# A decode block on one core: 4 MB loads in 5 slots, K^T stationary for the scores, stationary gate, up and down weights

## The chip, the cores and the metric

The kernel runs on one core of one Trainium2 chip. The metric is device time in microseconds (us), the median of repeated executions; lower is better. The runs of one kernel lie within about 0.3% of each other except for a few outliers. A profiled execution gives the trace. Its span, from the first to the last instruction, is some 1.8 us shorter than the measured time (before: 419.2 and 420.96).

Engines in the profile: PE is the matrix engine and PEld its loading of stationary operands, DVE and ACT are the vector and scalar engines, POOL is GpSimd, SP issues the large DMA transfers. The core has 16 DMA engines, and a transfer to all 128 partitions is spread over all 16 by its partitions.

## The reference

One token (`x`: 1 x 1024) goes through layer norm, attention over a cache of 65,536 positions with 32 query heads and 4 K/V heads of 128, an output projection with a residual, a second layer norm and a gated FFN with a residual.

```python
def _A_ref(x, k_cache, v_cache, wq, wo):            # k_cache, v_cache: 1 x 4 x 65536 x 128
    q = (x @ wq).reshape(1, 1, 32, 128).transpose(0, 2, 1, 3)
    k = jnp.repeat(k_cache, 8, axis=1); v = jnp.repeat(v_cache, 8, axis=1)
    p = softmax(jnp.einsum("bhqd,bhkd->bhqk", q, k) * 128 ** -0.5)
    o = jnp.einsum("bhqk,bhkd->bhqd", p, v)
    return o.transpose(0, 2, 1, 3).reshape(1, 1, 4096) @ wo
h  = x + _A_ref(layernorm(x), ...)
n  = layernorm(h)
h2 = h + (gelu(n @ w_gate) * (n @ w_up)) @ w_down   # 1024 -> 3584 -> 1024
```

Everything is bf16 in memory. K and V are 134 MB, all weights together 39 MB, and each byte is used once.

## The kernel before

Loads go through one pool of nine 2 MB slots. For every 1 MB of K ("chunk", 32 rows per partition) PE transposes the data as pairs of bf16 in 16 fp32 transposes, DVE and ACT copy the result out, and the scores are computed with the small query as stationary operand and K^T streaming by. The scores then lie along the free dimension and have to be transposed back.

```python
def k_chunk_QK(g, ci):
    ...
    for par in range(2):
        for c in range(NBK):                         # 8 matmuls, K^T moving, 512 columns each
            mv = kts[c][:]...rearrange("p (b k t) -> p b k t", b=NB2, t=2)
            nc.tensor.matmul(qk_ps[32 * c:32 * c + 32, :], lhsT=qsel[:, g, par, :], rhs=mv[:, :, :, par],
                             start=(par == 0), stop=(par == 1), tile_position=(0, 32 * c))
    nc.scalar.copy(out=qk_sb[:], in_=qk_ps[:])
    for b in range(NB2):                             # 4 transposes back
        nc.tensor.transpose(out=sct_ps[:, b, :], in_=qk_sb[:, b * P:(b + 1) * P], identity=ident_f[:])
    ...
```

The V products of head group g - 1 are issued between the chunks of K of group g. The FFN streams the weights past a small stationary operand, gets rows, and turns each row into columns by splitting it into a high and a low bf16 part and multiplying both by a vector of ones:

```python
for which, wmat in ((0, B_w_gate), (1, B_w_up)):
    ...
            wide_mm(r_ps, hnz, c0 + cc, DC, ...)     # weights moving, 512 columns
    ...
    nc.vector.tensor_tensor(out=g_lo[:, sl], in0=r_ps[s][:, 0:fw[s]], in1=g_hi[:, sl], op=ALU.subtract)
    for part in (g_hi, g_lo):
        for f in range(FC):                          # 2 x 28 matmuls turn the row
            nc.tensor.matmul(gu_ps[:, which, f:f + 1], lhsT=part[:, f:F:FC], rhs=ones_bf[:, 0:1], ...)
```

The down projection does the same for 16 of its 28 column blocks, and computes the other 12 with the weights stationary, the last one from a 256 KB load of its own.

## Time and profile before

| before | |
|---|---|
| time | 420.96 us (3 runs, 420.91 to 422.46) |
| span of the profiled run | 419.2 us |
| bytes loaded | 173.02 MB |
| DMA engines held by the load queue | 97.7% of the span |
| PE busy | 79% |

The windows view of before, cut to DMA. The columns are the stretch, its length, busy time of POOL (not used here), the clock granted to PE as a share of full speed (PEclk), the mean DMA share and GB/s.

```profile
core 0: us, POOL busy (x), PEclk, DMA share, GB/s
240.00:300.00 60.00, 0.00 (x0) 0.97 1.01 427
400.00:404.00 4.00, 0.00 (x0) 0.86 1.01 426
404.00:408.00 4.00, 0.00 (x0) 0.50 0.91 380
408.00:412.00 4.00, 0.00 (x0) 0.50 0.51 209
```

The 16 engines do not end together: the share falls to 0.91 and then to 0.51 over the last 8 us. The timeline of before shows what follows the last loads (start, length, what):

```profile
399.49 4.27 DVE L399 TENSOR_TENSOR g_lo<-gu_row_ps,g_hi 128x512 bf16<-128x512 f32 x7
...
403.81 1.94 PE L402 MATMUL gu_ps<-ones_bf,g_lo 128*128 128x1 bf16 x28 [2.18 <-DVE g_lo L399]
...
407.52 3.62 PE L340 MATMUL d_ps<-wd_sb,actz 128*32 128x512 bf16 x32 [1.76 <-issue]
...
413.41 2.70 PE L447 MATMUL dl_ps<-act_bf,wd_sb 128*128 128x1 bf16 x96
...
417.09 0.36 SPq L482 DMA_DIRECT2D out_dram<-o_row  x1
```

After the last up weights PE and DVE need until 407.5 us to have the operand of the down projection, and the down projection then goes on until 416.1. The last 2.1 us are the store. The last 96 matmuls start without a wait: in before it is this chain on PE and DVE, not the last load, that ends last.

### The profile page before, as it was taken

The numbers are of one execution on the slowest core, as the hardware profiler recorded it, in microseconds if no ns is written. First come the engines' busy times: TensorE is split into PE (matmuls) and PEld (weight loads), VectorE is DVE, ScalarE is ACT, GpSimd is POOL, SyncE is SP. The second block draws the span as 40 slices with busy tenths as digits, with TensorE's granted clock in tenths as the row PEclk, the third lists the DMA queues.
The fourth block names the chain that finished last, engine by engine and source line by source line (L and its number), as shares of the span: only waits on it lengthen the run. The fifth ranks groups of instructions, "written<-read, shape, count | busy, mean of one in ns | idle before, by whom it ended". The sixth has DMA issues, their size and how long they took to land.

```text
span 419.2 us, 7313 instructions
## 1 busy us (share of the span) xinstructions
PE 330.3 (79%) x3085; PEld 215.5 (51%) x3085; DVE 184.8 (44%) x370; ACT 187.2 (45%) x318; POOL 5.0 (1%) x15
## 2 busy tenths in 40 slices
PE   3339999997898887988889879898886674678845
PEld 2337676655555554655655555555563231434443
DVE  3014666662644564555554565545554010016162
ACT  1007676738565453845656555555563600001100
POOL 2000000000000000000000000000000100000000
PEclk9999999996999999899999989999999585557775
DMA  8999999999999999999999999999999999999991
GB/s 323 423 428 432 424 424 428 428 427 428 427 427 425 425 428 430 430 423 424 428 427 430 428 421 430 424 425 433 424 427 424 428 428 427 413 421 419 430 401 62
DMA packets 13840, 173.48 MB, mean 414 GB/s; under 512 B 1392, under 2 KB 1392, under 8 KB 3696
## 3 DMA queue, kind: packets, MB, share of 16 engines
q1 hardware_dynamic: 13792, 173.02, 97.7%
q8 instruction: 24, 0.39, 0.4%
q14 instruction: 8, 0.07, 0.0%
q10 hardware_dynamic: 16, 0.00, 0.0%
HBM read 173.02 MB, written 0.00 MB: 413 GB/s over the span
## 4 chain that ended last, share of the span: by engine, by line
PE 48%; DMA 19%; ACT 14%; DVE 13%; issue 4%; SPq 0%; ACTq 0%; DVEq 0%
PE kt_ps L193 22%; PE sct_ps L222 9%; PE qk_ps L216 8%; ACT kt_sb L199 7%; DMA wgu_sb<-in_B_w_up_dram 7%; DMA k_sb<-in_A_k_cache_dram 6%; DMA wo_sb<-in_A_wo_dram 6%; PE acc_ps L275 4%; DVE sc_sb L225 4%; ACT pT L255 4%; DVE kt_sb L201 3%; ACT qk_sb L219 3%; DVE mx L226 3%; DVE g_lo L399 1%; PE d_ps L340 1%
## 5 line engine op out<-in xcount | busy, mean ns | idle before, releaser
L199 ACT COPY kt_sb<-kt_ps 128x1024 bf16<-128x1024 bf16 x116 | 116.1, 1013 | 106.4 <-PE kt_ps L193 106.0
L193 PE MATMUL kt_ps<-ident_f,k_sb 128*128 128x128 f32 x1024 | 143.3, 286 | 11.5 <-DVE kt_sb L201 8.8
L193 PEld LDWEIGHTS kt_ps<-ident_f,k_sb 128*128 128x128 f32 x1024 | 117.3, 146 | 34.6 <-DVE kt_sb L201 16.0
L201 DVE COPY kt_sb<-kt_ps 128x1024 bf16<-128x1024 bf16 x140 | 94.3, 686 | 53.1 <-PE kt_ps L193 52.7
L225 DVE COPY sc_sb<-sct_ps 128x256 f32<-128x256 f32 x64 | 38.9, 608 | 72.7 <-PE sct_ps L222 72.5
L216 PE MATMUL qk_ps<-kt_sb,qsel 128*32 128x512 bf16 x512 | 66.5, 395 | 4.7 <-ACT kt_sb L199 3.8
L222 PE MATMUL sct_ps<-ident_f,qk_sb 128*128 128x128 f32 x256 | 41.7, 284 | 12.4 <-ACT qk_sb L219 9.6
L219 ACT COPY qk_sb<-qk_ps 128x512 f32<-128x512 f32 x64 | 37.7, 590 | 27.2 <-PE qk_ps L216 27.2
L222 PEld LDWEIGHTS sct_ps<-ident_f,qk_sb 128*128 128x128 f32 x256 | 27.3, 141 | 34.9 <-ACT qk_sb L219 27.5
L275 PE MATMUL acc_ps<-v_sb,pT 128*32 128x512 bf16 x512 | 42.7, 426 | 0.7 <-DMA v_sb<-in_A_v_cache_dram 0.7
L255 ACT ACTIVATE pT<-sc_sb,nbias 128x256 bf16<-128x256 f32 x64 | 31.5, 495 | 14.4 <-DVE nbias L248 14.4
L216 PEld LDWEIGHTS <-qsel 128*32 128x32 bf16 x512 | 15.9, 94 | 31.0 <-issue 26.7
L226 DVE TENSOR_REDUCE mx<-sc_sb 128x8 f32<-128x256 f32 x64 | 26.7, 417 | 1.6
L275 PEld LDWEIGHTS <-pT 128*32 128x32 bf16 x512 | 13.8, 104 | 17.2 <-issue 10.2
L340 PE MATMUL gu_row_ps<-wgu_sb,hnz 128*32 128x512 bf16 x112 | 20.7, 485 | 2.1 <-DVE hnz L332 1.5
L152 PE MATMUL q_ps<-xn_bf,wq_sb 128*128 128x1 bf16 x256 | 7.5, 165 | 13.6 <-DMA wq_sb<-in_A_wq_dram 13.6
L396 ACT CAST g_hi<-gu_row_ps 128x512 bf16<-128x512 f32 x6 | 3.1, 594 | 32.5 <-PE gu_row_ps L340 32.5
L340 PE MATMUL at_ps<-wo_sb,o2z 128*32 128x512 bf16 x64 | 7.6, 626 | 9.9 <-DMA wo_sb<-in_A_wo_dram 9.9
L340 PEld LDWEIGHTS <-hnz 128*32 128x32 bf16 x112 | 8.1, 114 | 12.8 <-issue 7.2
L152 PEld LDWEIGHTS <-wq_sb 128*128 128x128 bf16 x256 | 7.1, 104 | 13.9 <-DMA wq_sb<-in_A_wq_dram 13.9
L349 ACT COPY at_r<-at_ps 128x512 f32<-128x512 f32 x1 | 0.6, 586 | 30.4 <-PE at_ps L340 30.4
L394 DVE CAST g_hi<-gu_row_ps 128x512 bf16<-128x512 f32 x8 | 5.0, 684 | 19.8 <-PE gu_row_ps L340 19.8
(121 smaller groups left out, 109.9 us busy)
## 6 DMA issues: line engine op xcount, KB each, us to landing
k_sb<-in_A_k_cache_dram SPq DMA_DIRECT2D x32, 2048.0 KB, 23.3
v_sb<-in_A_v_cache_dram SPq DMA_DIRECT2D x32, 2048.0 KB, 22.9
wq_sb<-in_A_wq_dram SPq DMA_DIRECT2D x4, 2048.0 KB, 14.3
wo_sb<-in_A_wo_dram SPq DMA_DIRECT2D x4, 2048.0 KB, 24.5
wgu_sb<-in_B_w_gate_dram SPq DMA_DIRECT2D x4, 1792.0 KB, 32.4
wgu_sb<-in_B_w_up_dram SPq DMA_DIRECT2D x4, 1792.0 KB, 31.8
wd_sb<-in_B_w_down_dram SPq DMA_DIRECT2D x3, 2048.0 KB, 30.6
wd_sb<-in_B_w_down_dram SPq DMA_DIRECT2D x1, 768.0 KB, 32.1
```

Of the source, the lines that this page charges most:

```text
L152: nc.tensor.matmul(q_ps[:, h:h + 1], lhsT=w_sb[:, h * P:(h + 1) * P], rhs=xn_bf[:, c:c + 1], start=False, stop=False, skip_group_check=True)
L193: nc.tensor.transpose(out=kt_ps[:, b, :], in_=k32[:, n0:n0 + 2, :].rearrange("p t d -> p (t d)"), identity=ident_f[:])
L199: nc.scalar.copy(out=dst_bf, in_=src_bf)
L201: nc.vector.tensor_copy(out=dst_bf, in_=src_bf)
L216: nc.tensor.matmul(qk_ps[32 * c:32 * c + 32, :], lhsT=qsel[:, g, par, :], rhs=mv[:, :, :, par], start=(par == 0), stop=(par == 1), tile_po ...
L219: nc.scalar.copy(out=qk_sb[:], in_=qk_ps[:])
L222: nc.tensor.transpose(out=sct_ps[:, b, :], in_=qk_sb[:, b * P:(b + 1) * P], identity=ident_f[:])
L225: nc.vector.tensor_copy(out=dst_v, in_=src_v)
L226: nc.vector.tensor_reduce(out=st["mx"][:, :, ci], in_=sc_sb[:, :, ci * CH:(ci + 1) * CH], axis=AX.X, op=ALU.max)
L255: nc.scalar.activation(out=pT[:, a0:a1, r, :], in_=sc_sb[:, r, a0 * TG:a1 * TG].rearrange("p (a t) -> p a t", t=TG), func=ACT.Exp, bias=nb ...
L275: nc.tensor.matmul(acc[32 * c:32 * c + rep * TG, :], lhsT=pT[:, a, :, :].rearrange("p r t -> p (r t)"), rhs=v_sb[:, i * TG:(i + 1) * TG, : ...
L340: nc.tensor.matmul(ps[32 * g:32 * g + 32, 0:widths[s]], lhsT=stat[:, c, :], rhs=mov_of_slice(s), start=first, stop=last, tile_position=(0, ...
```

## The change

The intent is to load with longer rows (32 KB per partition and transfer), to make PE's work on the scores shorter, and to end the FFN without the split-and-turn step. The core of the diff:

```diff
-    CW = max(DCH * CH * Dh, 4096)     # 8192 columns: 2 MB
-    NBUF = 9 if DCH == 2 else 15
+    CW = 16384                        # 4 MB
+    NBUF = 5
...
-    wq_v = A_wq.rearrange("(c p) n -> p c n", p=P)
+    wq_v = A_wq.rearrange("(p c) n -> p c n", c=DC)     # model dim partition-major: rows of 32 KB
...
-        for par in range(2):
-            for c in range(NBK):
-                nc.tensor.matmul(qk_ps[32 * c:32 * c + 32, :], lhsT=qsel[:, g, par, :], rhs=mv[:, :, :, par], ...)
-        nc.scalar.copy(out=qk_sb[:], in_=qk_ps[:])
-        for b in range(NB2):
-            nc.tensor.transpose(out=sct_ps[:, b, :], in_=qk_sb[:, b * P:(b + 1) * P], identity=ident_f[:])
+        for c in range(NBK):
+            for b in range(NB2):
+                for par in range(2):                    # 32 matmuls, K^T stationary, 16 columns moving
+                    nc.tensor.matmul(sc_ps[:, c * NB2 + b, :], lhsT=kv[:, b, :, par], rhs=qsel[:, g, par, :], ...)
...
+    def up_proj(wmat, name, sizes):                     # gate and up: weights stationary, one moving column
+        wv_all = wmat.rearrange("(p c) n -> p c n", c=DC)
+        ...
+                for f in range(FC):
+                    nc.tensor.matmul(ps[:, f:f + 1], lhsT=wv[:, cc, f:F:FC], rhs=hn_bf[:, c0 + cc:c0 + cc + 1], ...)
...
+    sizes = [FC // 2, FC // 2 - 5, 4, 1]                # down: all 28 blocks with weights stationary
+            for j in range(DC):
+                nc.tensor.matmul(d_ps[:, j:j + 1], lhsT=wv[:, cc, j * P:(j + 1) * P], rhs=act_bf[:, c:c + 1], ...)
```

Cut out: the tile that holds the probabilities is split in two halves, the sum of the softmax is computed later, `x` is loaded in both layouts, and the pools are resized.

## The prediction

> **What bounds the kernel now.** The load stream. The page shows the load queue holding 97.7% of the 16 DMA engines' span; the windows view gives 426 to 428 GB/s from 22 to 334 us. The change reads the same 173.02 MB. PE is second (79% busy) and has the largest share of the chain of waits, but loads are issued early (median 23 us from issue to landing), so its waits do not reach the DMA. Time can be saved only in the rate, the start and the tail. In the windows the last weights land at about 411.8 us; the span ends at 419.2: a 7.4 us tail.
>
> **What the change does.**
> 1. Tail. Before, gate/up rows are split into high and low parts on DVE (2.5 + 4.3 us), turned by 56 matmuls (3.9), then follow 32 wide down matmuls (3.6), another split, and 96 small ones (2.7). After, gate, up and down are 224 small matmuls each. Contiguous stationaries take 28 ns here (96 in 2.70 us), step 28 takes 68 ns (28 in 1.9 us, at granted clock 0.5 and 1.0 alike). So gate and up need 15.2 us each and down 6.3, against about 17 us of loading each: PE keeps up. After the last 256 KB: 8 matmuls (0.4), add (0.2), transpose (0.4), copy (0.3), store to end (2.1), about 3.6 us. Gain about 3.8 us, all critical.
> 2. Rate. Rows of 16 KB run at 427 GB/s, 8 KB (wq) at 424, 7 KB (gate, up) at 420. Extrapolating a fixed cost per packet, 32 KB should give 428 to 430: an estimate of 1 to 3 us in all. The Trainium skill ("DMA: Bandwidth & Descriptors", Where 436 GB/s comes from) gives a ceiling of 435 GB/s; this trace is at 98% of it.
> 3. Scores. Per 1 MB of K, 8 wide matmuls, 4 transposes and a copy (1.04 + 0.65 us PE, 0.59 ACT) become 32 matmuls with K^T stationary, step 2. The skill ("SBUF — State Buffer", SBUF "cachelines") says bf16 steps inside a 16-byte line are free; no run shows it yet, but 68 ns at step 28 agrees. I expect about 30 ns, 0.95 us. PE gets lighter by 0.7 us per 1 MB, off the critical path.
> 4. Granularity. 20 MB in 5 slots instead of 18 MB in 9: slots free later. My estimate leaves about 6 us at the tightest place (the softmax after the first head group), so no DMA gap. PE instructions double (3,633 to 7,261 rows in the order view); fetching them costs about 1 us of DMA at most.
>
> Sum: 3.8 + 2 + 0 - 0.5, about 5 to 6.5 us less.
>
> **Prediction: 414.7 us, 80% range 410 to 419.5.** Faster by over 2%: 0.27; within 2%: 0.66; slower by over 2%: 0.07.
>
> **What would show it.** Last weight landing to the end: 3.5 to 4 us. DMA at 428 to 430 GB/s in attention. Score matmuls near 30 ns apart, gate and up about 68. DMA share 1.0 until some 4 us before the end, no dip at 90 to 115 us.
>
> **What would make it wrong.** Step-2 stationaries costing 60 ns or more: PE would take about 4.2 us per 1 MB of K in the first group against 3.45 now, and slots would free late, with tens of us of DMA gaps at worst. Late slots at the softmaxes anyway. 32 KB rows at 432 GB/s or more, or slower than 16 KB ones. The 16 engines finish unevenly (share 0.5 in the last 4 us); that might shrink or grow.

## More of the kernel before

The lines of the page of before: the span, the busy share of PE, the DMA engines and their GB/s in 40 slices of 10.5 us, the queues (packets, MB, share of 16 engines' time), and the groups of the scores and of the transposes back (count, then busy us and mean ns, then idle time and what ended it).

```profile
span 419.2 us, 7313 instructions
...
PE 330.3 (79%) x3085; PEld 215.5 (51%) x3085; DVE 184.8 (44%) x370; ACT 187.2 (45%) x318; POOL 5.0 (1%) x15
...
DMA  8999999999999999999999999999999999999991
GB/s 323 423 428 432 424 424 428 428 427 428 427 427 425 425 428 430 430 423 424 428 427 430 428 421 430 424 425 433 424 427 424 428 428 427 413 421 419 430 401 62
...
q1 hardware_dynamic: 13792, 173.02, 97.7%
q8 instruction: 24, 0.39, 0.4%
...
L216 PE MATMUL qk_ps<-kt_sb,qsel 128*32 128x512 bf16 x512 | 66.5, 395 | 4.7 <-ACT kt_sb L199 3.8
L222 PE MATMUL sct_ps<-ident_f,qk_sb 128*128 128x128 f32 x256 | 41.7, 284 | 12.4 <-ACT qk_sb L219 9.6
```

DMA is full from the second slice to the last but one, mostly at 420 to 430 GB/s (413 to 433, and 401 in the last but one). PE is busy too, but loads are issued some 23 us ahead, so what PE waits for does not reach the DMA. The q8 line passes easily unnoticed: 24 packets that are not data but instructions.

## The result, and the profile after

| | before | after |
|---|---|---|
| time | 420.94 us (4 runs, 420.68 to 422.46) | 417.44 us (4 runs, 417.31 to 417.52) |
| ratio | | 0.9907 (95% interval 0.9889 to 0.9925) |
| span | 419.2 us | 415.6 us |
| matmuls (each with a weight load of its own, so two PE instructions) | 3,085 | 4,685 |

Ratios are the mean time of one kernel's fast runs over that of the other's fast runs of the same rounds, so they are not quite the ratio of the medians quoted. The change saves 3.5 us, 0.9%.

The page of after, the same lines:

```profile
span 415.6 us, 10378 instructions
...
PE 305.7 (74%) x4685; PEld 267.0 (64%) x4685; DVE 163.3 (39%) x343; ACT 146.2 (35%) x247; POOL 4.2 (1%) x13
...
DMA  8999999999999999999999999999999999999992
GB/s 353 420 435 445 412 439 418 434 424 432 427 431 428 431 427 435 417 434 427 437 418 444 413 443 415 442 423 434 428 422 446 416 445 416 425 434 422 437 383 104
...
q1 hardware_dynamic: 6496, 173.02, 97.3%
q8 instruction: 36, 0.59, 0.6%
...
L210 PE MATMUL sc_ps<-qsel,kt_sb 128*128 128x16 bf16 x2048 | 74.0, 170 | 10.2 <-ACT kt_sb L192 10.2
...
L353 PE MATMUL wg_ps<-hn_bf,wg_sb 128*128 128x1 bf16 x224 | 14.3, 202 | 1.2 <-DVE hn_bf L135 1.2
```

The scores take PE 74.0 us in 2,048 small matmuls, where before they took 66.5 us in 512 wide ones and another 41.7 us for the transposes back. The load queue now has 6,496 packets instead of 13,792 and the same bytes. The instruction queue has 36 packets instead of 24. The windows of after:

```profile
core 0: us, POOL busy (x), PEclk, DMA share, GB/s
240.00:300.00 60.00, 0.00 (x0) 0.89 1.00 429
400.00:404.00 4.00, 0.00 (x0) 0.50 0.93 388
404.00:408.00 4.00, 0.00 (x0) 0.50 0.54 225
408.00:412.00 4.00, 0.00 (x0) 0.50 0.29 115
```

The DMA share falls earlier (0.54 in 404 to 408 us, where before had 0.91), yet some engines work on past 408. The timeline of the end of after:

```profile
388.72 14.32 PE L353 MATMUL wu_ps<-hn_bf,wu_sb 128*128 128x1 bf16 x224
...
403.33 3.25 PE L385 MATMUL d_ps<-act_bf,wd_sb 128*128 128x1 bf16 x112 [0.28 <-DVE act_bf L373]
...
408.76 2.08 PE L385 MATMUL d_ps<-act_bf,wd_sb 128*128 128x1 bf16 x72 [2.18 <-DMA wd_sb<-in_B_w_down_dram]
...
411.27 1.23 PE L385 MATMUL d_ps<-act_bf,wd_sb 128*128 128x1 bf16 x40 [0.43 <-DMA wd_sb<-in_B_w_down_dram]
...
413.52 0.35 SPq L395 DMA_DIRECT2D out_dram<-o_row  x1
```

The down projection waits for its loads and ends at 412.5 us; before it ended at 416.1.

The rest of this section is from the trace's records of DMA completions, which no view prints. Each of these loads adds 1 to its semaphore from each of the 16 engines, and only the sixteenth means that it has landed. The Trainium skill says so in "DMA: Bandwidth & Descriptors" (Why a DMA increments its semaphore by 16 and not by 1). For the last 256 KB of weights, the first of the 16 came at the time in the second column, and the others so much later:

```
         first    the 16 engines, us after the first                                             last
before   407.5    0 0.3 0.3 0.4 0.4 0.8 3.0 3.1 3.3 4.6 4.7 4.7 4.8 4.9 4.9 4.9                   412.5
after    403.7    0 0.1 0.3 0.3 0.3 0.9 2.3 4.0 6.3 6.4 6.6 6.6 6.7 7.9 8.0 8.2                   411.9
```

The first engine is done 3.8 us earlier than before, the last one only 0.6 us. From the last landing to the end of the span it was 6.7 us before and is 3.7 us now. These two are the whole result: 0.6 + 3.0 = 3.6 us of span. The question is why 3.2 us of the 3.8 us that the loads gained were lost at the last engine.

The offsets come in steps of about 1.6 us, and they grow during the run: in after the spread of a load's 16 completions is 0.5 us until the first instruction packet at 23 us, 2.0 us after it, 3.6 us after 9 such packets, 5.1 us after 17, 6.7 us after 26 and 8.2 us after 33. In before it is 4.9 us at the end, after 23. In both traces the 16 KB instruction packets take 0.9 to 1.5 us each. That suggests theory F: instruction packets go in turn to 8 of the 16 engines, each sets its engine back by about 1.6 us, and the kernel ends with the most burdened engine. 23 packets are at most 3 per engine (3 x 1.63 = 4.9 us), 36 at most 5 (8.2 us). Two further engines end in between (2.3 and 4.0 us in after); they fall back in smaller steps, at about the times of some 8 KB packets of another instruction queue (q14), which no run varies.

Two packet times belong to it, also from the trace's packet records: the median 16 KB load packet took 614 ns in before, the median 32 KB packet 1,215 ns in after. One long packet is 13 ns shorter than two short ones, and an engine moves 288 of them, 256 of K and V and 16 each of wq and wo, which makes 3.7 us. This is theory R, for the earlier first engine. It is an estimate: gate, up and down are left out, and wq had 8 KB rows in before. The completions give less: the first engine finishes a 4 MB load every 9.711 us in after and a 2 MB load every 4.893 us in before (medians), which over 36 loads of 4 MB makes 2.7 us.

The rivals: the uneven end has another cause (L); the lighter scores are part of the gain (P); longer loads do nothing and the new tail is all (the rival of R).

### The profile page after: what moved, and what is told of

Same layout as the page of the kernel before. It is cut to its first block, busy times and chain, and to the rows that moved or that the text cites. A ratio compares the mean times of both kernels' runs of the same rounds, so it can differ in the third digit from the quotient of the medians.

```text
span 415.6 us, 10378 instructions
## 1 busy us (share of the span) xinstructions
PE 305.7 (74%) x4685; PEld 267.0 (64%) x4685; DVE 163.3 (39%) x343; ACT 146.2 (35%) x247; POOL 4.2 (1%) x13
## 3 DMA queue, kind: packets, MB, share of 16 engines
q1 hardware_dynamic: 6496, 173.02, 97.3%
## 4 chain that ended last, share of the span: by engine, by line
DMA 37%; PE 37%; issue 18%; ACT 4%; DVE 2%; POOL 0%; SPq 0%; POOLq 0%; ACTq 0%
DMA k_sb<-in_A_k_cache_dram 34%; PE kt_ps L187 21%; PE sc_ps L210 5%; DMA wd_sb<-in_B_w_down_dram 4%; PE acc_ps L258 4%; PE wg_ps L353 3%; ACT kt_sb L192 2%; ACT pT L241 2%; PE wu_ps L353 2%; PE o_ps L274 1%; PE l_ps L267 0%; PE bc_ps L231 0%; DVE acc_sb L271 0%; PE d_ps L385 0%; PE mxT_ps L225 0%
## 5 line engine op out<-in xcount | busy, mean ns | idle before, releaser
L187 PE MATMUL kt_ps<-ident_f,k_sb 128*128 128x128 f32 x1024 | 150.5, 303 | 26.7 <-DMA k_sb<-in_A_k_cache_dram 26.7
L187 PEld LDWEIGHTS kt_ps<-ident_f,k_sb 128*128 128x128 f32 x1024 | 129.1, 157 | 29.8 <-issue 28.8
L210 PEld LDWEIGHTS <-kt_sb 128*128 128x128 bf16 x2048 | 70.3, 97 | 19.3 <-ACT kt_sb L192 13.0
L210 PE MATMUL sc_ps<-qsel,kt_sb 128*128 128x16 bf16 x2048 | 74.0, 170 | 10.2 <-ACT kt_sb L192 10.2
L214 DVE COPY sc_sb<-sc_ps 128x256 f32<-128x256 f32 x64 | 38.3, 601 | 19.7 <-PE sc_ps L210 19.5
L353 PEld LDWEIGHTS <-wg_sb 128*128 128x128 bf16 x224 | 14.5, 173 | 1.2 <-issue 1.2
L353 PE MATMUL wg_ps<-hn_bf,wg_sb 128*128 128x1 bf16 x224 | 14.3, 202 | 1.2 <-DVE hn_bf L135 1.2
L353 PE MATMUL wu_ps<-hn_bf,wu_sb 128*128 128x1 bf16 x224 | 14.3, 202 | 0.0
L353 PEld LDWEIGHTS <-wu_sb 128*128 128x128 bf16 x224 | 14.3, 172 | 0.0
L241 ACT ACTIVATION_READ_ACCUMULATOR pT<-sc_sb,nbias 128x1 f32 x64 | 11.9, 186 | 0.0
## 6 DMA issues: line engine op xcount, KB each, us to landing
wu_sb<-in_B_w_up_dram SPq DMA_DIRECT2D x1, 3584.0 KB, 41.7
```

Of the source, the lines that this page charges most:

```text
L187: nc.tensor.transpose(out=kt_ps[:, b, :], in_=k32[:, c * NB2 + b, :], identity=ident_f[:])
L210: nc.tensor.matmul(sc_ps[:, c * NB2 + b, :], lhsT=kv[:, b, :, par], rhs=qsel[:, g, par, :], start=(par == 0), stop=(par == 1))
L214: nc.vector.tensor_copy(out=dst_v, in_=src_v)
L241: nc.scalar.activation(out=pT[:, :, r, :], in_=sc_sb[:, r, hf * HG * TG:(hf + 1) * HG * TG].rearrange("p (a t) -> p a t", t=TG), func=ACT. ...
L353: nc.tensor.matmul(ps[:, f:f + 1], lhsT=wv[:, cc, f:F:FC], rhs=hn_bf[:, c0 + cc:c0 + cc + 1], start=False, stop=False, skip_group_check=True)
```

## The experiments

All versions gave correct results. Ratios are to before; a second table below has the landings. The differences of 1 to 3 us read below are larger than the noise: within after, loads2mb, newtail, qkwide and widegu the spans of all runs agree within 0.3 us.

### 1. Smaller loads: loads2mb

```diff
-    CW = 16384
-    NBUF = 5
+    CW = 8192
+    NBUF = 10
...
-    sizes = [FC // 2, FC // 2 - 5, 4, 1]
+    sizes = [8, 8, 7, 4, 1]
```

> after with 2 MB loads in 10 slots (16 KB rows, as before) in place of 4 MB in 5; all else the same but the cuts of the up and down weights. Theory R (longer packets are the rate gain): packets of 16 KB take 614 ns and of 32 KB 1,215 ns, so two cost 13 ns more than one; some 290 packets of 32 KB per engine give about 3.8 us, so the time rises by 3 to 4 us to about 421, as slow as before. The spread stays near 8.2 us (36 fetches). Rival: the size of loads does nothing and the gain is all in the tail: time within 0.5 us of after.

Measured: 420.83 us, ratio 0.9996 (0.9981 to 1.0011). The first engine ended at 406.8 us, 3.1 us later than in after, the last at 414.8 with a spread of 8.0. The page of loads2mb:

```profile
span 418.6 us, 10462 instructions
...
q1 hardware_dynamic: 12400, 173.02, 97.6%
q8 instruction: 36, 0.59, 0.6%
```

With 2 MB loads the rest of the change is worth nothing. So the longer rows are worth 3.4 us in time and 3.1 us at the first engine, between the two sums of theory R (2.7 from completions, 3.7 from packets), and the 36 instruction packets cost the same with either size. The number of loads and slots changed along with the rows; no run separates them.

### 2. The old scores: qkwide

```diff
-        for c in range(NBK): ... 32 matmuls, lhsT=kv[:, b, :, par]
+        ... the 8 wide matmuls, the ACT copy and the 4 transposes of before
-    ktpool bufs=5, ps_kt bufs=4, ps_sc bufs=2
+    ktpool bufs=6, qkpool bufs=1, ps_kt bufs=3, ps_qk bufs=2, ps_sct bufs=1
```

> after with the old scores: K^T moving, 8 wide matmuls and 4 transposes in place of 32 matmuls with K^T stationary. That takes away 1,280 matmuls, so about 26 fetches instead of 36. Theory F: at most 4 on one engine, spread 6.6 us instead of 8.2, time 1.6 us less than after (about 415.8), though PE is busier. Rival P (lighter PE work in attention is part of the gain): slower than after, by DMA gaps when slots free late; K work per 1 MB goes up from about 3.0 to 3.5 us, so the tightest slot has some 2 us left instead of 13.

Measured: 415.67 us, ratio 0.9884 (0.9862 to 0.9905), faster than both kernels. The page and the windows of qkwide:

```profile
PE 325.8 (79%) x3405; PEld 231.9 (56%) x3405; DVE 171.6 (41%) x343; ACT 183.1 (44%) x311; POOL 4.2 (1%) x13
...
q8 instruction: 26, 0.43, 0.4%
```

```profile
core 0: us, POOL busy (x), PEclk, DMA share, GB/s
404.00:408.00 4.00, 0.00 (x0) 0.50 0.60 246
408.00:412.00 4.00, 0.00 (x0) 0.50 0.06 20
```

PE is busier than in after (325.8 us against 305.7) and the kernel is 1.8 us faster (all four spans are 413.7 to 413.9 us, also that of the one run that took 417.24; in after they are 415.5 to 415.7). The last landing came at 410.1 us as predicted (403.7 + 4 x 1.63 = 410.2). The spread was 5.1 and not 6.6 us, because the first engine landed at 405.0 instead of 403.7: the leading engines, which are ahead of the others, ran out of issued loads for about 1 us near 270 us. So rival P is right in this much, that the heavier scores use up the slack of the slots; but that only reached engines that would have waited anyway (the last landings stay 9.7 us apart there). Here the 10 saved instruction packets are worth more than the 20 us of PE time.

### 3. Padding with matmuls that nothing reads: pad400, pad800, padv

```diff
+    pad_ps = ps_m.tile([P, 1], F32, name="pad_ps", tag="misc")
+    for _ in range(400):                 # or 800
+        nc.tensor.matmul(pad_ps[:], lhsT=ident_bf[:], rhs=ident_bf[:, 0:1], start=True, stop=True)
     q_ps = ps_m.tile([P, Hq], F32, name="q_ps", tag="misc")
```

> 400 small matmuls on the identity are added before the q projection, in the time in which PE waits for the first weights; nothing reads them. Theory F (instruction fetches): the trace of after has 36 instruction packets of 16 KB for 4,685 matmuls, they rotate over 8 of the 16 DMA engines, each sets its engine back by about 1.6 us, and the last load waits for the most burdened engine (5 fetches, landing 8.2 us after the first of the 16). 400 more matmuls give 39 fetches, still at most 5 on one engine: spread 8.2 us, time unchanged within 0.3 us. Rival L (the engines end unevenly for another reason, such as load sizes): also unchanged, spread 8.2. A smooth cost per instruction would give about +0.7 us.

> The same with 800. Theory F: 42 fetches, two engines get a sixth, so the spread of the landings becomes 9.8 us and the time rises by about 1.6 us against after, although the added matmuls lie in an idle stretch of PE. Rival L: no change, as PE has 6 us to spare before the first K load lands and the loads are the same.

Measured: 419.1 us with 400 (ratio 0.9956, 0.9939 to 0.9973) and 432.81 us with 800 (1.0266, 1.0235 to 1.0297). Both miss what theory F expected. The design was at fault. The timeline of pad800 shows PE on the padding:

```profile
17.42 5.95 PE L148 MATMUL pad_ps<-ident_bf 128*128 128x1 bf16 x218 [1.18 <-DVE x_cp L144]
25.57 3.57 PE L148 MATMUL pad_ps<-ident_bf 128*128 128x1 bf16 x128 [2.19 <-issue]
32.04 3.58 PE L148 MATMUL pad_ps<-ident_bf 128*128 128x1 bf16 x128 [2.90 <-issue]
...
54.52 5.63 PE L154 MATMUL q_ps<-xn_bf,wq_sb 128*128 128x1 bf16 x206 [0.22 <-DVE q_ps L150]
```

After the first 218 and then after every 128 small matmuls, that is 256 PE instructions or one 16 KB packet, PE waits 2.2 to 3.4 us for "issue", and the padding takes 36.9 us, until 54.3, where 800 matmuls of 28 ns would take 22. The q projection comes late, the first slots come free late, and the windows of pad800 have a DMA share of 0.02 from 52 to 56 us. The spread at the end was only 6.3 us with 42 packets (the page counts a 43rd, after the last landing), and 6.3 us with 39 in pad400; that the burdened engines catch up when the loads pause is the likely reason. So these two runs say nothing for or against theory F; they show that PE can starve for instructions when the load queue is full. A new version puts the padding where PE waits for loads:

```diff
+        if g == Hkv - 1:                 # between the V products of the last head group
+            for _ in range(32): nc.tensor.matmul(pad_ps[:], lhsT=ident_bf[:], rhs=ident_bf[:, 0:1], start=True, stop=True)
...
+            if wc == 0:                  # first half of the output projection
+                for _ in range(8): nc.tensor.matmul(pad2_ps[:], lhsT=ident_bf[:], rhs=ident_bf[:, 0:1], start=True, stop=True)
```

> A second try at the padding, where it can not delay the first head group: 512 small matmuls on the identity between the V products of the last head group and 128 in the first half of the output projection, in which PE waits for loads anyway. 5,325 matmuls, 41 fetches. Theory F: one engine gets a sixth fetch, landings 8.2 + 1.6 = 9.8 us apart, time about 1.6 us more than after (419.0), with a DMA share of 1.0 up to 400 us. Rival L: unchanged at 417.4.

Measured: 418.78 us, ratio 0.9935 (0.9916 to 0.9954); the four runs were 418.76, 418.80, 418.88 and 417.48. In the profiled run all 8 burdened engines had 5 packets (offsets 7.8 to 8.2 us) for the last load but one, with a spread still of 8.2; the 41st packet came just before the last load and put one engine 1.6 us further back, to 413.5 us. The last load was issued 1.4 us later than in after, and so the first engine came 1.3 us later (405.0 us); but the other seven burdened engines landed at 411.5 to 411.9, so the late issue is not what made the one late. The fourth run has the time of after; that it had no sixth packet in time was not seen, as it was not profiled. The page of padv counts the packets:

```profile
q8 instruction: 41, 0.67, 0.7%
```

Four more packets cost nothing and the fifth cost 1.3 us: this is what a maximum over engines looks like, and rival L, which expected 417.4, falls.

### 4. The new tail alone: newtail

```diff
 (before, up to and including the attention part)
-    ... output projection, gate, up and down of before
+    ... output projection, gate, up and down of after, with sizes = [8, 8, 7, 4, 1] and loads of 2 MB
```

> before up to the output projection (2 MB loads, old scores), then the new one of after: gate, up and down as column products. Theory F and R: 16 KB rows, so an engine without fetches lands its last bytes near 407.5 us as in before; 3,397 matmuls give 26 or 27 fetches, at most 4 on one engine, so the last landing comes at 407.5 + 4 x 1.63 = 414.0; from there 3.7 us as in after: span 417.7, time about 419.5, 1.5 us less than before. If the tail were the whole of the gain and fetches cost nothing, the time would be 3.0 us less than before, about 418.0.

Measured: 419.69 us, ratio 0.9961 (0.9944 to 0.9977). First landing 407.2, last 413.7, then 3.8 us to the end. The new tail takes 2.9 us off the end, and its 320 additional matmuls put 1.2 us of it back on the slowest engine.

### 5. Giving the burdened engines less to load: offload, offload2, qkwide_off

```diff
+    for i in range(16):                                   # offload: 6 blocks, 8 partitions at a time
+        nc.sync.dma_start(out=wv[8 * i:8 * i + 8], in_=wd_v[8 * i:8 * i + 8, 0:6, :])
```

> after, but 6 of the 28 down-weight columns are loaded by 16 transfers of 8 partitions each, which run on 8 of the 16 DMA engines only; the other loads are unchanged. 1.5 MB go to 8 engines, so each of those gets 98 KB (3.6 us at the measured 27 GB/s) more than an even share and the other 8 as much less. Theory F, if these 8 are the engines without the fetches: their last landing moves from 403.7 to about 407.3 and that of the 8 burdened ones from 411.9 to about 408.3, the spread shrinks from 8.2 to some 2 us and the time falls by about 3 us to 414.4. If they are the burdened ones: the last landing moves to about 415.5 and the time rises by 3 to 4 us. If fetches rotate over all engines: rises by less than 3.6 us with a spread of 4 to 8 us.

Measured: 426.93 us, ratio 1.0154 (1.0105 to 1.0203). The timeline of SP in offload:

```profile
381.67 18.73 SPq L386 DMA_DIRECT2D wd_off<-in_B_w_down_dram  x16
400.87 2.11 SPq L77 DMA_DIRECT2D wd_sb<-in_B_w_down_dram  x3
```

This missed too: issuing the 16 transfers took 18.7 us, and the large loads behind them were issued 19 us late, with a gap in the DMA. Why the issue is slow was not tried. A mend with 4 transfers, issued early:

```diff
+    for np_ in (49, 49, 21, 9):                           # offload2: 5 blocks
+        nc.sync.dma_start(out=woff[p0:p0 + np_], in_=wd_v[p0:p0 + np_, 0:5, :])
+        p0 += np_
```

> A mend of the first offload, which kept the DMA-issuing engine waiting 18.7 us for its 16 small transfers. Now 5 down-weight columns (1.31 MB) come in 4 transfers of 49, 49, 21 and 9 partitions into a buffer of their own, issued before the up weights; if a transfer of n partitions runs on the largest divisor of n up to 16 engines, these use 7, 7, 7 and 9. In the first offload the small transfers began at 386 us, when only the engines without fetches were free, so they should fall on those. Theory F: the burdened engines lose 82 KB each (3.0 us) and land last at about 408.9 instead of 411.9; the others land at about 407. PE then ends its own chain at 409.5 at best, so the time falls by 1.5 to 2.8 us to 414.6 to 416. If the uneven ends are not what bounds the kernel: no change or slower.

> Both remedies: old scores (26 fetches, last landing 410.1 in the earlier run) and the same 4 transfers. Theory F: burdened engines land at about 407, the others at about 408; PE, whose gate, up and down products take 14.3 + 14.3 + 6.4 us from 374 on, is then what ends last, near 409.6, so span about 412.9 and time about 414.7, 1 us less than the old scores alone and 6.3 us less than before. If DMA is still the end: 413.5 or less is not reached and the time stays near 415.7.

Measured: 432.72 us for offload2 (ratio 1.0277, 1.0252 to 1.0301) and 428.71 us for qkwide_off (1.0178, 1.0162 to 1.0194). Both miss. The windows of offload2 while the 4 transfers ran:

```profile
core 0: us, POOL busy (x), PEclk, DMA share, GB/s
384.00:388.00 4.00, 0.00 (x0) 0.50 1.00 227
388.00:392.00 4.00, 0.00 (x0) 0.50 0.96 226
```

The DMA share is full and the rate is half. The 10 KB packets of these transfers took from 0.39 us to over 1.0 us, mostly 0.6 to 0.8, where 10 KB at the rate of the long packets would be 0.38. A likely reason is in the Trainium skill, "SBUF — State Buffer" (Door 1: The DMA port swizzle): DMA reaches the SBUF through 16 ports, and partitions 0 to 63 lie behind only 8 of them. The page gives 196 GB/s for a 1 MiB transfer to these 64 partitions and 328 for all 128. The first of the transfers here goes to partitions 0 to 48. No run here isolates that.

The completions also show that the premise failed. The transfers did run on few engines (8 in offload; 7, 7, 7 and 9 in offload2), but not only on those without instruction packets: the first one of offload landed on its 8 engines at 387.6 us (three of them), 389.4, 391.1, 393.6, 395.2 and 395.8, so three were 6 to 8 us behind, as only burdened engines are. In this form it costs more than it gives, and whether the load can be balanced stays open.

### 6. Still fewer instructions, and the old gate and up alone: fewer, widegu

```diff
 (widegu: after; fewer: qkwide)
-    def up_proj(...): ... 224 matmuls each for gate and up, weights stationary
+    def up_proj(...): ... 56 wide matmuls each, split in high and low, 56 turning matmuls, as in before
```

> A version to beat both: 4 MB loads and the new down product of after, but the old scores and the old wide gate and up products (split in high and low parts and turned). 3,181 matmuls, some 24 or 25 fetches, so 3 on each of 8 engines, perhaps 4 on one. Theory F: last landing at 403.4 + 3 x 1.63 = 408.3 (409.9 with a fourth), then 3.7 us: span 412.0 to 413.6, time 413.8 to 415.4. If fetches were not the cause of the late end: 415.7 as with the old scores alone. If the longer chain from the last up weights to the down product (some 12 us in before) ends last: above 416.

> after with the old wide gate and up products only: 4,461 matmuls, 34 or 35 fetches, still 5 on the most burdened engines. Theory F, which counts the most burdened engine: last landing 411.9 as in after, time unchanged at 417.4 within 0.4 us, although two fetches fewer are made and PE is busy for a shorter time. A cost per instruction would give 0.4 us less; if the new gate and up products are what shortens the tail, it would be slower by up to 3 us.

Measured: fewer 416.91 us, ratio 0.9902 (0.9887 to 0.9917); widegu 418.3 us, 0.9935 (0.9917 to 0.9953). In widegu 34 of the 35 packets that the page counts were begun before the last landing, and left the most burdened engine with 5: last landing 411.6 against 411.9 in after, as theory F says. In fewer 24 of 25 brought the last landing down to 409.4, within the range expected. Yet both times missed what theory F alone expected (417.4 and 413.8 to 415.4), and neither is faster than the version that it was made from (after 417.44, qkwide 415.67), because PE ends last now, which the expectations had named as the other case. The timeline of fewer:

```profile
399.23 1.92 PE L389 MATMUL wu_ps<-ones_bf,g_hi 128*128 128x1 bf16 x28 [2.04 <-DVE g_hi L381]
403.33 1.94 PE L389 MATMUL wu_ps<-ones_bf,g_lo 128*128 128x1 bf16 x28 [2.18 <-DVE g_lo L386]
405.55 5.23 PE L420 MATMUL d_ps<-act_bf,wd_sb 128*128 128x1 bf16 x191 [0.28 <-DVE act_bf L407]
```

The up rows are split and turned until 405.3 us, and the down products follow without waiting for a load until 412.3. So the stationary gate and up weights are worth something beyond instruction counts: without them PE, not the DMA, ends the kernel, 0.9 us later in widegu and 1.2 us later in fewer than with them.

### All landings

"Packets" are the 16 KB instruction packets that the page counts; landings are those of the last 256 KB of weights; "after it" is from the last landing to the end of the span.

| kernel | matmuls | packets | first engine | last engine | spread | after it | time |
|---|---|---|---|---|---|---|---|
| before | 3,085 | 24 | 407.5 | 412.5 | 4.9 | 6.7 | 420.94 |
| after | 4,685 | 36 | 403.7 | 411.9 | 8.2 | 3.7 | 417.44 |
| loads2mb | 4,685 | 36 | 406.8 | 414.8 | 8.0 | 3.8 | 420.83 |
| newtail | 3,405 | 26 | 407.2 | 413.7 | 6.5 | 3.8 | 419.69 |
| padv | 5,325 | 41 | 405.0 | 413.5 | 8.5 | 3.5 | 418.78 |
| widegu | 4,461 | 35 | 403.6 | 411.6 | 8.0 | 5.0 | 418.30 |
| qkwide | 3,405 | 26 | 405.0 | 410.1 | 5.1 | 3.7 | 415.67 |
| fewer | 3,181 | 25 | 405.4 | 409.4 | 3.9 | 6.0 | 416.91 |

The last engine of a kernel with 32 KB rows is at about 403.7 + 1.63 us times the packets of its most burdened engine (6, 5, 5, 4 for padv, after, widegu, qkwide: 413.5, 411.9, 411.9, 410.2). With 16 KB rows it is 407 instead of 403.7. In fewer, with 3, the sum gives 408.6 and 409.4 was measured; there all engines, the last one too, were held up by 0.9 us or more near 195 us.

## Why the prediction was right or wrong

The time was predicted at 414.7 us with a range of 410 to 419.5, and "within 2%" as the likeliest; 417.44 lies in the range. The gain was 3.5 us where 5 to 6.5 were expected. By its terms, tail 3.8, rate 2 and fetching -0.5 were forecast and 3.0, 3.8 and -3.3 measured: the rate was underrated by 1.8 us and the fetching by 2.8, and that the two errors partly cancel is luck.

- *The bound.* Right. The load stream bounds both kernels up to their tails; a version that makes PE busier (qkwide) is faster, and one that shortens the rows (loads2mb) loses everything.
- *Tail, 3.8 us.* Right in kind, 3.0 us measured. The new tail was expected at 3.6 us and took 3.7. The error is in the old one: I read the last landing off the falling DMA share as 411.8 us, while the sixteenth completion came at 412.5.
- *Rate, 1 to 3 us, 428 to 430 GB/s.* Right in kind, too low in us: the windows give 429 GB/s for 240 to 300 us, an engine without instruction packets ends 3.8 us earlier, and undoing the size alone costs 3.4 us. The skill's ceiling of 435 GB/s ("DMA: Bandwidth & Descriptors", Where 436 GB/s comes from) is not contradicted by any mean over a long window.
- *Scores, 30 ns each, off the critical path.* Right: in the timeline of after, 33 of them take 0.97 us, 29 ns each, at step 2 (the step is the distance in elements from one column of the stationary operand to the next). The skill's rule on 16-byte lines ("SBUF — State Buffer", SBUF "cachelines") fits both this and the 64 ns at step 28 (gate: 224 in 14.3 us). That the lighter PE work is worth nothing by itself is shown by qkwide.
- *Granularity.* Right: no DMA gap in after.
- *Instruction fetch, "about 1 us of DMA at most".* This is the term that was mis-sized. Spread over 16 engines, 12 additional packets of about 1.1 us would be 0.8 us per engine. In the trace they fall on 8 engines, each costs its engine 1.6 us rather than the 1.1 us that it lasts (why is open), and the last engine counts, not the mean one: 2 more packets on the most burdened engine, 3.3 us. 3.8 us gained by rate less 3.3 us leaves 0.5 us; measured at the last landing: 0.6. The count was not the fault: the prediction had PE instructions double, and they rose by half, from 6,170 to 9,370.
- *"DMA share 1.0 until some 4 us before the end."* Wrong by the same step: it is 0.93 from 400 to 404 us and 0.54 from 404 to 408, 8 to 12 us before the end. The prediction did name the uneven end as a risk, without a cause.

## What to carry to other kernels

When a kernel is bound by its loads, count PE instructions as load traffic: here each 256 of them are one 16 KB packet that sets one DMA engine back by 1.6 us, and the kernel ends with the engine that got most of them. Many small matmuls in place of a few wide ones may shorten PE's work and still lengthen the kernel; the best version here takes the long rows and the new tail and leaves the scores wide (415.67 us against 420.94 and 417.44). And look for the last completion of a transfer rather than the mean DMA share before you say when the loads end.

## What the Trainium skill lacked or had wrong

- "Runtime: NRT & Kernel Launch" (Instruction fetch mechanics) says that instructions come in 16 KiB blocks of 256 and that crossing a block costs "one DMA tail-bump, mostly hidden". The size agrees (after has 2 x 4,685 = 9,370 PE instructions, a matmul and a stationary load each; 9,370 / 256 = 36.6, and 36 packets of 16 KB), the cost does not: with the load queue full each block set one DMA engine back by 1.6 us, 8.2 us on the last engine of after.
- The same section holds that fetching is hidden because instructions are dispatched more slowly than they are filled. In pad800 PE stopped for 2.2 to 3.4 us after every 128 small matmuls beside a full load queue.
- No page says on which DMA engines the instruction packets run. Here they fell on 8 of the 16 (in padv 40 of them put exactly 8 engines back by 7.8 to 8.2 us).
- "DMA: Bandwidth & Descriptors" gives this chip's load rates by transfer size but not by row length. Here load packets took 275 ns for 7 KB, 309 for 8 KB, 614 for 16 KB and 1,215 for 32 KB.
- The same page describes the engines' round-robin between queues by packet, but not what it can do to a tiny load: `x` in rows of 16 bytes, 2 KB in all, took 12.3 us to land in after and 7.3 us in loads2mb. Row length is not the whole cause: in qkwide and widegu, with 32 KB rows too, its packets started just ahead of the load queue's and were through by 6.6 us. It cost nothing that was seen, as the first K landed at 34 us.
